# Moving a batch's transposes from the MLP's first half to the output product, with norm statistics as separate steps and a reordered first batch

## The chip, the cores and the metric

The kernel runs on one core of one Trainium2 chip (trn2). The metric is device time in microseconds (us) of one execution. Engines are named as in the profile: PE is TensorE, PEld its weight loads, DVE is VectorE, ACT is ScalarE, POOL is GpSimd. "PEclk" is the granted TensorE clock, where 1.00 is full speed. Most executions of one kernel agree to a few tenths of a per cent. A few are slow: of the kernel before, one took 393.4 us. Only fast runs are compared here.

## The reference, cut to what matters

Dilated sliding-window attention over 8 batches and 8 heads is followed by a gated MLP with a spatial gating unit. Heads 0 to 3 look at the last 32 positions ("plain" heads), and heads 4 to 7 at every fourth of the last 128 ("dilated" heads).

```python
# q, k, v: [8 batches, 8 heads, 576, 64]
scores = scale * q @ k.T;  scores = where(masks, scores, -1e9)
attn = softmax(scores);    x = (attn @ v)            # -> [8, 576, 512]
h = gelu(x @ w_in)                                   # 512 -> 1024
u, v = h[..., :512], h[..., 512:]
v_n = (v - mean(v)) / sqrt(var(v) + 1e-6) * g_ln     # norm over the 512 features
v_s = einsum('ts,bsd->btd', w_sg, v_n) + b_sg        # mixes the positions of a batch
out = x + (u * v_s) @ w_out
```

`w_sg` mixes all positions, so the gating product of a batch cannot finish before the last rows of `v_n` exist.

## The kernel before

The program is written as a list of steps for each batch. Each engine gets its instructions in the order in which the steps stand, so a text of step names is the schedule. `T` transposes q and k, `S` makes scores, `AV` the weighted values, `X` transposes the attention output, `zv`/`zu` are the MLP's first half for v and u, `vn` the norm, `sgu` the gating product, and `out` the output product. In iteration `p`, attention of batch `p` runs beside the gating and output of batch `p - 1`.

```python
ps = tc.tile_pool(name="ps", bufs=4, space=PSUM)       # four PSUM tiles [128, 2, 512] FP32 for everything
NKT, NPT = 3, 10                                       # buffers for kT and for PT

def a_T(b, g):                        # transposes of one head pair
    pq, pk = psum("pq"), psum("pk")
    ...                               # 12 to 16 matmuls against the identity
    nc.scalar.copy(qT, pq[:, :, 0:HS])
    nc.scalar.copy(k0, pk[0:64, :, 0:HS])
    nc.vector.tensor_copy(k1, pk[64:128, :, 0:HS])     # 0.76 us on DVE

def a_S(b, h):
    ...                                                # scores, then Exp on ACT into PT
    eng = nc.gpsimd if b and h % 4 == 3 else nc.vector # masks of heads 3 and 7 on POOL
    eng.tensor_tensor(PT[:, 0:S], PT[:, 0:S], masks[:, h // 4], AO.mult)

def m_zv(b, i):
    ...                                                # 8 matmuls, Gelu on ACT into vv
    for c in range(n):
        nc.vector.bn_stats(st[:, c, :], vv[:, c, :])
        nc.vector.bn_aggr(mv[:, c, :], st[:, c, :])
    nc.gpsimd.tensor_scalar_add(rs[:, 0:n], mv[:, 0:n, 1:2], 1e-6)
    nc.gpsimd.tensor_tensor(rs[:, 0:n], rs[:, 0:n], mhalf[:, 0:n], AO.pow)

def m_vn(b, i):
    for c, ti in enumerate(tis):
        nc.vector.tensor_scalar(vn[:, ti, :], vv[:, c, :], mv[:, c, 0:1],
                                rs[:, c, :], AO.subtract, AO.mult)
...
    # iteration p; io is a list of loads, spread evenly over the steps of a run
    io = ...                                           # v of batch p + 1
    run("S:0 sgu:0 S:1 S:2 sgu:1 S:3 S:4 sgu:2 S:5 sgu:3 S:6 S:7 gelu", env, io)
    run("AV:0 vd AV:1 out:0 X:0 AV:2 X:1 out:1 AV:3 X:2 T:0 X:3 out:2", env, ...)
    io = LOADS["qk"](p + 2) if p + 2 < B else []
    run("zv:0 T:1 zv:1 vn:0 W:0 T:2 zv:2 vn:1 W:1 zu:0 vn:2 T:3 zu:1 W:2 zu:2 W:3 zu:3 W:4",
        env, io)                                       # W prepares w_sg in iteration 0 only
```

Note that the statistics of `vv` follow each `zv` at once, while `vn` stands one `zv` later. Between them DVE has other work: the next statistics and the casts of kT for the transposes `T:1` and `T:2`. All loads are issued by POOL, which also computes `rs`, the reciprocal standard deviation.

The softmax here doesn't subtract the row's maximum and nothing guards it: scores larger than these inputs give would overflow.

## Time and profile before

| | before |
|---|---|
| median (lowest) of its three fast runs | 290.62 us (288.78) |
| profiled execution: span, mean granted clock | 287.8 us, 0.972 |
| first MLP product of batch 0 | 31.13 us |
| first product of batch 1 | 72.60 us |
| five periods from batch 1 to batch 6 | 158.3 us, so 31.7 each |
| batch 6 to batch 7 (no more loads or transposes) | 31.0 us |
| tail from batch 7's first product to the end | 25.9 us |

I cut the execution at the first product of each batch, the matmul that begins `zv:0`. The distance from one to the next is called the period. From the page of the kernel before come the busy time of each engine and the shares of the chain of work that ended last, by engine.

```profile
PE 234.7 (82%) x2494; PEld 167.4 (58%) x2494; DVE 198.7 (69%) x380; ACT 179.2 (62%) x265; POOL 138.9 (48%) x189
...
DVE 31%; PE 30%; ACT 13%; DMA 10%; POOL 8%; issue 6%; POOLq 0%; ACTq 0%; DVEq 0%
```

The view by windows of the kernel before gives the same stretches as the table. The columns are: start and end, length, busy us and number of instructions of PE, PEld, DVE, ACT and POOL, then the granted clock, the DMA share and GB/s.

```profile
0.00:31.13 31.13, 15.34 (x189) 13.80 (x189) 19.89 (x51) 15.41 (x24) 22.65 (x33) 0.92 1.44 147
31.13:72.60 41.47, 33.77 (x340) 22.89 (x339) 27.43 (x49) 22.59 (x34) 23.00 (x32) 0.90 1.26 140
72.60:230.90 158.30, 139.06 (x1543) 99.43 (x1541) 118.11 (x216) 111.56 (x165) 83.95 (x111) 1.00 0.85 101
230.90:261.93 31.03, 27.01 (x299) 19.41 (x297) 22.08 (x43) 21.25 (x31) 5.94 (x8) 1.00 0.11 39
261.93:287.80 25.87, 19.55 (x135) 11.90 (x132) 11.22 (x23) 8.43 (x12) 3.37 (x6) 0.96 0.15 52
```

In the third row PE is busy for 139 of 158 us (88%) at full clock. It is the fullest engine, but not always busy, and DVE leads the chain.

In the timeline of DVE, batch 3 of the kernel before, each line is start, duration, engine, line, operation, operands and count. In brackets stand the idle time before it and what ended that.

```profile
140.77 0.76 DVE L224 CAST kT<-pk 64x576 f16<-64x576 f32 x1
141.56 0.69 DVE L324 BATCH_NORM_STATS2 st<-vv 128x6 f32<-128x512 f32 x1
...
143.19 0.97 DVE L334 TENSOR_SCALAR vn<-vv,mv,rs 128x512 f16<-128x512 f32 x2
144.19 0.81 DVE L224 CAST kI<-pk 64x576 f16<-64x576 f32 x1
...
148.66 0.55 DVE L334 TENSOR_SCALAR vn<-vv,mv,rs 128x512 f16<-128x512 f32 x1 [1.46 <-POOL rs L327]
...
150.11 0.46 DVE L250 TENSOR_TENSOR PT<-PT,masks 128x576 f16<-128x576 f16 x1
```

The kT casts at 140.77 and 144.19 and the second statistics at 141.56 fill the time in which POOL computes `rs`. Only the last `vn` waits (1.46 us), because POOL was issuing four loads, from 144.68 to 147.7, before that `rs`. It runs at 148.66, 12.66 us after the batch's first product at 136.00. The timeline of PE in the same stretch shows what depends on it.

```profile
136.00 1.89 PE L315 MATMUL pz<-w_in,xT 128*128 128x512 f16 x8
...
149.26 0.91 PE L357 MATMUL pv<-wsgT,vn 128*128 128x288 f16 x6 [1.09 <-DVE vn L334]
...
150.60 1.39 PE L357 MATMUL pv<-wsgT,vn 128*128 128x288 f16 x10
...
157.34 0.81 PE L374 MATMUL po<-w_out,gat 128*128 128x512 f16 x3 [0.37 <-DVE vs L361]
```

PE gets to the gating product (`pv`) early, does four of its ten matmuls, and waits 1.09 us for the last `vn`. The output product `po` begins at 157.34, 21.34 us after the first product. The steady batch can be described by three numbers: last `vn` at 12.66, `out:0` at 21.34, next batch at 31.70 us.

### The profile page before, as it was taken

What the parts mean: (1) busy time and instruction counts of PE and PEld (TensorE: products, weight loads), DVE (VectorE), ACT (ScalarE), POOL (GpSimd) and SP (SyncE); (2) the same over time, 40 slices, a digit from 0 to 9 for tenths busy, and PEclk for the clock granted to TensorE, in tenths of its full rate; (3) what the DMA queues carried; (4) which work ended last, traced back from release to release, by engine and by line L of the source; (5) the groups of instructions that cost most, each with busy time, mean ns of one, the idle gap of its engine ahead of it and who ended that gap; (6) DMA issues with size and microseconds to landing.
All of it is one profiled execution on the core that took longest, in us unless ns stands there. A gap on an engine that the chain in (4) does not pass through costs nothing.

```text
span 287.8 us, 6135 instructions
## 1 busy us (share of the span) xinstructions
PE 234.7 (82%) x2494; PEld 167.4 (58%) x2494; DVE 198.7 (69%) x380; ACT 179.2 (62%) x265; POOL 138.9 (48%) x189
## 2 busy tenths in 40 slices
PE   0467957898889798888889898879889889888883
PEld 0366634766468466666567656756566647754652
DVE  7548347795579839794679748993879557973760
ACT  1366643656786478756787478665876678745502
POOL 8953828481188606890198407970396013200400
PEclk9998777999999999999999999999999999999998
DMA  9999999998169921997079923995099310012004
GB/s 129 133 190 150 155 183 108 103 107 151 53 43 126 184 99 8 95 159 171 18 48 156 156 93 25 108 147 155 16 69 164 122 57 2 2 73 93 0 0 164
DMA packets 91467, 28.92 MB, mean 100 GB/s; under 512 B 71664, under 2 KB 86064, under 8 KB 91440
## 3 DMA queue, kind: packets, MB, share of 16 engines
q0 software_dynamic: 85232, 18.48, 72.3%
q1 hardware_dynamic: 6208, 10.06, 10.3%
q8 instruction: 19, 0.31, 0.4%
q14 instruction: 8, 0.07, 0.1%
HBM read 37.54 MB, written 9.44 MB: 163 GB/s over the span
## 4 chain that ended last, share of the span: by engine, by line
DVE 31%; PE 30%; ACT 13%; DMA 10%; POOL 8%; issue 6%; POOLq 0%; ACTq 0%; DVEq 0%
PE po L374 8%; PE pu L344 8%; DVE vs L361 7%; PE pz L315 7%; DVE gat L364 5%; DVE st L324 5%; DMA w_in<-in_moe_w_in_dram 4%; DVE PT L250 4%; DMA wsg<-in_moe_w_sg_dram 4%; DVE onorm L273 3%; ACT vv L319 3%; POOL kp L123 2%; ACT u L347 2%; PE po L377 2%; ACT osb L380 2%
## 5 line engine op out<-in xcount | busy, mean ns | idle before, releaser
L326 POOL TENSOR_SCALAR rs<-mv 128x2 f32<-128x2 f32 (+1 forms) x24 | 7.2, 300 | 96.8 <-DVE mv L325 96.1
L357 PE MATMUL pv<-wsgT,vn 128*128 128x288 f16 x320 | 45.4, 286 | 7.3 <-DVE vn L334 6.3
L247 ACT ACTIVATE PT<-pss 128x576 f16<-128x576 f32 x64 | 38.5, 650 | 16.5 <-PE pss L243 9.9
L374 PE MATMUL po<-w_out,gat 128*128 128x512 f16 x160 | 42.6, 379 | 5.6 <-DVE gat L364 3.0
L324 DVE BATCH_NORM_STATS2 st<-vv 128x6 f32<-128x512 f32 x40 | 27.2, 681 | 25.2 <-ACT vv L319 24.8
L315 PE MATMUL pz<-w_in,xT 128*128 128x512 f16 x160 | 39.9, 392 | 5.6 <-DVE kT L224 5.6
L380 ACT COPY osb<-po 128x1024 f32<-128x1024 f32 (+1 forms) x24 | 20.9, 870 | 37.4 <-issue 20.9
L357 PEld LDWEIGHTS <-vn 128*128 128x128 f16 x320 | 29.0, 97 | 16.2 <-DVE vn L334 8.6
L344 PE MATMUL pu<-xT,w_in 128*128 128x288 f16 x256 | 35.7, 294 | 2.6 <-ACT u L347 1.6
L344 PEld LDWEIGHTS <-w_in 128*128 128x128 f16 x256 | 25.7, 100 | 11.6 <-issue 3.7
L334 DVE TENSOR_SCALAR vn<-vv,mv,rs 128x512 f16<-128x512 f32 x40 | 22.1, 584 | 13.8 <-POOL rs L327 13.8
L273 DVE TENSOR_TENSOR onorm<-poa,rc 96x768 f16<-96x768 f32 (+1 forms) x32 | 30.6, 956 | 1.1
L319 ACT ACTIVATE vv<-pz 128x1024 f32<-128x1024 f32 (+1 forms) x24 | 21.1, 882 | 14.0 <-PE pz L315 11.6
L347 ACT ACTIVATE u<-pu 128x576 f16<-128x576 f32 x32 | 20.8, 651 | 13.2 <-PE pu L344 13.1
L123 POOL DMA_DIRECT2D qp<-in_q_dram x32 | 25.1, 786 | 6.8 <-DMA wsg<-in_moe_w_sg_dram 3.7
L215 ACT CAST qT<-pq 128x576 f16<-128x576 f32 x32 | 20.4, 638 | 12.3 <-PE pq L204 6.4
L123 POOL DMA_DIRECT2D kp<-in_k_dram x32 | 23.9, 752 | 7.8 <-DMA w_in<-in_moe_w_in_dram 4.1
L315 PEld LDWEIGHTS <-xT 128*128 128x128 f16 x160 | 15.3, 101 | 20.9 <-issue 7.5
L361 DVE SCALAR_TENSOR_TENSOR vs<-pv,g_col,b_bc 128x576 f16<-128x576 f32 x32 | 25.9, 811 | 1.2 <-PE pv L357 1.0
L250 POOL TENSOR_TENSOR PT<-PT,masks 128x576 f16<-128x576 f16 x14 | 17.8, 1273 | 18.2 <-ACT PT L247 18.2
L374 PEld LDWEIGHTS <-gat 128*128 128x128 f16 x160 | 14.4, 100 | 18.9 <-DVE gat L364 7.2
L250 DVE TENSOR_TENSOR PT<-PT,masks 128x576 f16<-128x576 f16 x50 | 21.9, 452 | 4.1 <-ACT PT L247 3.3
(65 smaller groups left out, 442.1 us busy)
## 6 DMA issues: line engine op xcount, KB each, us to landing
out_dram<-osb SPq DMA_DIRECT2D x32, 256.0 KB, 2.3
qp<-in_q_dram POOLq DMA_DIRECT2D x32, 72.0 KB, 3.9
kp<-in_k_dram POOLq DMA_DIRECT2D x32, 72.0 KB, 3.4
qd<-in_q_dram POOLq DMA_DIRECT2D x8, 288.0 KB, 5.5
kd<-in_k_dram POOLq DMA_DIRECT2D x8, 288.0 KB, 6.5
vp<-in_v_dram POOLq DMA_DIRECT2D x8, 288.0 KB, 8.4
vm<-in_v_dram POOLq DMA_DIRECT2D x8, 256.0 KB, 6.5
vt<-in_v_dram POOLq DMA_DIRECT2D x16, 96.0 KB, 6.1
```

Source lines behind the costliest of these rows:

```text
L123: nc.gpsimd.dma_start(dst, src)
L247: nc.scalar.activation(PT[:, 0:S].rearrange("p (j w) -> p j w", j=2), pss[:, :, 0:HS], AF.Exp, scale=0.125)
L250: eng.tensor_tensor(PT[:, 0:S], PT[:, 0:S], masks[:, h // 4], AO.mult)
L273: nc.vector.tensor_tensor(onorm.rearrange("p a h d -> p h a d"), pv[:, :, :, 0:64], rc.unsqueeze(3).broadcast_to([rows, 2, NB, 64]), AO.mult)
L315: nc.tensor.matmul(pz[:, c, :], xT[:, g4, MT[ti]:MT[ti] + 128], w_in16[:, g4, DH:DFF], start=(g4 == 0), stop=(g4 == 3))
L319: nc.scalar.activation(vv[:, 0:n], pz[:, 0:n], AF.Gelu_apprx_tanh)
L324: nc.vector.bn_stats(st[:, c, :], vv[:, c, :])
L344: nc.tensor.matmul(pu[:, j, 0:HS], w_in16[:, g4, 128 * ph:128 * ph + 128], xT[:, g4, HS * j:HS * j + HS], start=(g4 == 0), stop=(g4 == 3))
L357: nc.tensor.matmul(pv[:, j, 0:HS], vn[:, kp, 128 * ph:128 * ph + 128], wsgT16[:, kp, HS * j:HS * j + HS], start=(kp == 0), stop=(kp == 4))
L361: nc.vector.scalar_tensor_tensor(vs.rearrange("p (j w) -> p j w", j=2), pv[:, :, 0:HS], g_col[:, ph:ph + 1], b_bc.rearrange("p (j w) -> p ...
L374: nc.tensor.matmul(po[:, c, :], gat[:, ph, ts], w_out16[:, ph, :], start=(ph == 0), stop=False)
L380: nc.scalar.copy(osb[:, 0:n], po[:, 0:n])
```

## The change

The intent has four parts. All transposes of the next batch move out of the MLP's first half and stand beside the output product. The statistics become a step of their own (`st`), so that DVE's order can be chosen freely. Batch 0 begins with the dilated heads, whose load is one large transfer each for q and k. Loads become named steps, and three masks per batch (heads 0, 2, 4) go to POOL instead of two. Some buffers are reduced too (`NKT` and `NPT` in the cut, and `xT` from four to two); e14_best3 below keeps these fewer buffers and is faster than the kernel before, so they alone do not make a kernel slow.

```diff
-    NKT = 3
+    NKT = 2
-    NPT = 10
+    NPT = 8
...
-        dma(w_in16, moe_w_in.rearrange("(g p) f -> p g f", p=128))
+        for half in (slice(DH, DFF), slice(0, DH)):
+            dma(w_in16[:, :, half], moe_w_in[:, half].rearrange("(g p) f -> p g f", p=128))
...
-        eng = nc.gpsimd if b and h % 4 == 3 else nc.vector
+        eng = nc.gpsimd if b and h in (0, 2, 4) else nc.vector
...
+        norm[b, i] = (vv, tis)
+
+    def m_st(b, i):                       # bn_stats, bn_aggr, and rs on POOL, moved here
+        vv, tis = norm.pop((b, i))
...
-    for f, *a in LOADS["qk"](0) + LOADS["v"](0):
+    for f, *a in [(ld_dil, 0), (ld_vd, 0), (ld_plain, 0, 0), (ld_plain, 0, 2),
+                  (ld_vp, 0, 0, 4), (ld_win,), (ld_plain, 1, 0), (ld_plain, 1, 2), (ld_dil, 1)]:
...
+            run("""T0:2 T0:3 S:4 S:5 S:6 S:7 vd T0:0 AV:2 T0:1 AV:3 S:0 X:2 S:1 X:3 S:2 S:3
+                   AV:0 AV:1 gelu X:0 X:1
+                   zv:0 zv:1 st:0 vn:0 zv:2 st:1 vn:1 st:2 wsg LV LVd wout zu:0 vn:2 zu:1 T:0 zu:2
+                   T:1 zu:3 T:2 W:0 W:1 T:3 W:2 W:3 W:4""", env)          # iteration 0
...
-        run("S:0 sgu:0 S:1 S:2 sgu:1 S:3 S:4 sgu:2 S:5 sgu:3 S:6 S:7 gelu", env, io)
-        run("AV:0 vd AV:1 out:0 X:0 AV:2 X:1 out:1 AV:3 X:2 T:0 X:3 out:2", env, io)
-        run("zv:0 T:1 zv:1 vn:0 W:0 T:2 zv:2 vn:1 W:1 zu:0 vn:2 T:3 zu:1 W:2 zu:2 W:3 zu:3 W:4",
-            env, io)
+        run("S:0 S:1 sgu:0 S:2 S:3 sgu:1 S:4 S:5 sgu:2 S:6 sgu:3 S:7 gelu", env)
+        if p == 1:
+            for f, *a in [(ld_plain, 2, 0), (ld_plain, 2, 2), (ld_dil, 2)]:
+                f(*a)
+        run("vd AV:0 LV AV:1 T:0 out:0 X:0 AV:2 LVd X:1 T:1 out:1 AV:3 X:2 T:2 LD X:3 T:3 out:2", env)
+        run("zv:0 st:0 zv:1 vn:0 st:1 zv:2 vn:1 st:2 zu:0 vn:2 LP:0 zu:1 LP:2 zu:2 zu:3", env)
```

In the new text, `LP` and `LD` load q and k of batch `p + 2` (plain heads, dilated heads), and `LV` and `LVd` load v of batch `p + 1`.

More of the change, by code (lines that the diff above doesn't have):

```diff
@@ L108, in setup_consts @@
         nc.sync.dma_start(masks, MSK.ap())
-        nc.vector.memset(mhalf, -0.5)
         for i in range(NKT):
@@ L112, in setup_consts @@
                 nc.vector.memset(kTs[i][hd], 0.0)
-            nc.vector.memset(kIs[i], 0.0)
-        for t in vps + vds:
-            nc.vector.memset(t[0:HALO], 0.0)
-            nc.vector.memset(t[:, :, :, 64:65], 1.0)
+        for t in kIs:
+            nc.vector.memset(t, 0.0)
+        for i in range(NV):
+            nc.vector.memset(vps[i][0:HALO, 0, 0, 0:D], 0.0)
+            nc.vector.memset(vps[i][:, :, :, D:D + 1], 1.0)
+            nc.vector.memset(vds[i][:, :, :, D:D + 1], 1.0)
         for t in PTb:
             nc.vector.memset(t[:, S:PTW], 1.0)
+        nc.vector.memset(mhalf, -0.5)
         nc.vector.memset(wsgT16[0:64, 4, :], 0.0)
@@ L127, in open_batch @@
     def open_batch(b):
+        if b in loaded:
+            return
         qp = ld.tile([QB, NB, 4, D], FP16, tag="qp", name="qp")
@@ L134, in ld_plain @@
     def ld_plain(b, h0):
-        if h0 == 0:
-            open_batch(b)
+        open_batch(b)
         for t, src in zip(loaded[b][0], (q, k)):
@@ L141, in ld_dil @@
     def ld_dil(b):
+        open_batch(b)
         for t, src in zip(loaded[b][1], (q, k)):
@@ L279, in a_X @@
         onorm = onorms.pop((b, g))
-        if g == 0:
-            xTs[b] = sb.tile([128, 4, S], FP16, tag="xT", name="xT", bufs=4)
+        if b not in xTs:
+            xTs[b] = sb.tile([128, 4, S], FP16, tag="xT", name="xT", bufs=2)
         xT = xTs[b]
@@ L319, in m_zv @@
         nc.scalar.activation(vv[:, 0:n], pz[:, 0:n], AF.Gelu_apprx_tanh)
+        norm[b, i] = (vv, tis)
+    def m_st(b, i):
+        vv, tis = norm.pop((b, i))
+        n = len(tis)
         st = sb.tile([128, 2, 6], FP32, tag="st", name="st", bufs=3)
@@ L387, in gelu_table, with run @@
         nc.scalar.activation(warm, mhalf[:, 0, :], AF.Gelu_apprx_tanh)
-    LOADS = {"qk": lambda b: [(ld_plain, b, 0), (ld_plain, b, 2), (ld_dil, b)],
-             "v": lambda b: [(ld_vp, b, 0, 4), (ld_vd, b)]}
-    def run(text, env, io):
-        steps = text.split()
-        done = 0
-        for i, step in enumerate(steps):
-            while done < len(io) and done * len(steps) <= i * len(io):
-                f, *a = io[done]
-                f(*a)
-                done += 1
+    def run(text, env):
+        for step in text.split():
             name, _, n = step.partition(":")
@@ L404, in run @@
                 f(*a, *([int(n)] if n else []))
-        for f, *a in io[done:]:
-            f(*a)
     setup_consts()
-    for f, *a in LOADS["qk"](0) + LOADS["v"](0):
+    for f, *a in [(ld_dil, 0), (ld_vd, 0), (ld_plain, 0, 0), (ld_plain, 0, 2),
+                  (ld_vp, 0, 0, 4), (ld_win,), (ld_plain, 1, 0), (ld_plain, 1, 2), (ld_dil, 1)]:
         f(*a)
-    ld_win()
-    for g in range(4):
-        a_T(0, g)
     for p in range(B + 1):
@@ L417 @@
             env |= {"S": (a_S, p), "AV": (a_AV, p), "X": (a_X, p), "vd": (cp_vd, p),
-                    "zv": (m_zv, p), "vn": (m_vn, p), "zu": (m_zu, p)}
+                    "zv": (m_zv, p), "st": (m_st, p), "vn": (m_vn, p), "zu": (m_zu, p)}
         if p + 1 < B:
-            env["T"] = (a_T, p + 1)
-        if p == 0:
-            env["W"] = (prep_wsg,)
+            env |= {"T": (a_T, p + 1), "LV": (ld_vp, p + 1, 0, 4), "LVd": (ld_vd, p + 1)}
+        if p + 2 < B:
+            env |= {"LP": (ld_plain, p + 2), "LD": (ld_dil, p + 2)}
         if p >= 1:
@@ L425 @@
         if p == 0:
-            io = LOADS["qk"](1) + [(ld_wsg,)]
-        else:
-            io = LOADS["v"](p + 1) if p + 1 < B else []
-        run("S:0 sgu:0 S:1 S:2 sgu:1 S:3 S:4 sgu:2 S:5 sgu:3 S:6 S:7 gelu", env, io)
-        io = LOADS["v"](1) + [(ld_wout,)] if p == 0 else []
-        run("AV:0 vd AV:1 out:0 X:0 AV:2 X:1 out:1 AV:3 X:2 T:0 X:3 out:2", env, io)
-        io = LOADS["qk"](p + 2) if p + 2 < B else []
-        run("zv:0 T:1 zv:1 vn:0 W:0 T:2 zv:2 vn:1 W:1 zu:0 vn:2 T:3 zu:1 W:2 zu:2 W:3 zu:3 W:4",
-            env, io)
+            env |= {"T0": (a_T, 0), "W": (prep_wsg,), "wsg": (ld_wsg,), "wout": (ld_wout,)}
+            run("""T0:2 T0:3 S:4 S:5 S:6 S:7 vd T0:0 AV:2 T0:1 AV:3 S:0 X:2 S:1 X:3 S:2 S:3
+                   AV:0 AV:1 gelu X:0 X:1
+                   zv:0 zv:1 st:0 vn:0 zv:2 st:1 vn:1 st:2 wsg LV LVd wout zu:0 vn:2 zu:1 T:0 zu:2
+                   T:1 zu:3 T:2 W:0 W:1 T:3 W:2 W:3 W:4""", env)
+            continue
+        run("S:0 S:1 sgu:0 S:2 S:3 sgu:1 S:4 S:5 sgu:2 S:6 sgu:3 S:7 gelu", env)
[4 more added lines that the diff above has]
+        run("zv:0 st:0 zv:1 vn:0 st:1 zv:2 vn:1 st:2 zu:0 vn:2 LP:0 zu:1 LP:2 zu:2 zu:3", env)
 _INS = ['q', 'k', 'v', 'moe_w_in', 'moe_g_ln', 'moe_w_sg', 'moe_b_sg', 'moe_w_out']
```

## The prediction

> **What bounds the kernel now.** The busy table by windows gives a steady batch (first product to first product) of 31.7 us: PE 27.8, DVE 23.7, ACT 22.3, POOL 17.4 busy. PE leads, but the timeline shows where it waits. Counted from the first MLP matmul of a batch: MLP's first half ends at 11.3; `sgu:0` waits for the last `vn` until 13.2 (idle 1.1); S/sgu ends at 19.7; AV/X/out at 31.7, with DVE working without a break from 14.1 to 26.9, `out:0` waiting for `gat` and `X:1` for `onorm`. Batch 0 reaches its first product at 31 us and batch 1 at 72.8 (chain of waits: DMA of `w_in`, then of `wsg`). Six periods follow (to 262.1), then a 25.7 us tail.
>
> **What the change does.**
> 1. First half without transposes: PE 8.2 us of work instead of 9.8. But DVE's order becomes st0 vn0 st1 vn1 st2 vn2, and each vn waits for POOL's `rs` (add 0.23, pow 0.73, plus hand-over: 1.15 us). Before, st1 and the kT casts covered that. Walk: vv0 at 3.0, st0 4.7, vn0 6.9, st1 8.6, vn1 10.9, st2 11.7, vn2 13.4. So `sgu:0` starts no earlier than today (13.2); PE just idles longer (some 4 us).
> 2. The eight q/k loads LP stand on POOL between the last `rs` (12.8) and the first mask. At 0.73 each POOL is busy until 18.7, then masks h0, h2, h4 at 1.27 each until 22.6. AV:0 waits until about 20, AV:1 until 21.5.
> 3. In the trace, `gat` on DVE takes 1.2 us instead of 0.46 wherever it overlaps a POOL mask. The Trainium skill, "SBUF — State Buffer", section "Who interferes with whom", says that a DVE instruction with two SBUF inputs contends with a GpSimd instruction that reads SBUF; the trace agrees. Three masks in a row will now hold up gat2, gat3 and DVE's own masks, about 1 to 2 us.
> 4. `out:0` now comes after AV:0, AV:1 and T:0, which fill all four PSUM tiles, so it waits for AV:0's onorm, behind `vd` (0.75): 23 without item 3's delays, up to 26.3 with them, against 21.3 today. From there PE needs 10.4 us to the next first product, three more transposes included. Period 33.4 to 36.7 instead of 31.7.
>
> **On the critical path:** items 1 to 4, in the five periods with a full set of loads and transposes: +1.8 to +5 us each. Batch 6 to 7 stays near 31. The tail gains item 1's exposed waits: +3.3.
>
> **Start.** Dilated loads first, AV and X between: first product at about 23 instead of 31. But `wsg` is issued after the last `rs` (about 36), lands near 41.5, and five `W` with DVE evictions follow: the first `sgu` near 47 instead of 53. Batch 2's loads are issued after batch 1's masks, so T:0 waits for them. Batch 1's first product at about 71 (-2).
>
> Sum: 71 + 5 x 35.5 + 31 + 29 = about 309 us, slower by 6%. Range 298 to 321. Faster 0.05, same 0.1, slower 0.85.
>
> **Right if** the windows show steady periods of 33 to 37 us, vn waiting for POOL rs some 1.1 us three times a batch, the first mask on POOL starting behind the qp/kp issues, PE idle before `sgu:0` and before `out:0`, and the first product near 23. Longer PE idleness may also lower the clock: before, matmuls ran at about half speed around 42 to 50 us after such a gap (the skill's "TensorE: Matmul & The Clock Gate", Part 1, gives an idle window as cause).
>
> **Wrong if** DVE covers the rs waits, POOL's issues are cheaper than 0.73 us, PSUM tiles come free in another order, or the 8 us gained at the start survive `wsg` and steady batches stay under 32.5.

## More of the kernel before

The groups of waits in the kernel before have the columns total us, times and longest us.

```profile
DVE vn L334 <- POOL rs L327: 13.8, 8, 5.5
...
PE pv L357 <- DVE vn L334: 6.3, 7, 1.1
```

## The result, and the profile after

The changed kernel is correct and took 332.05 us (median of four fast runs, 331.36 to 332.86) against 290.62 us for the kernel before (median of its three fast runs, 288.78 to 291.59; the fourth was the slow one). The ratio is 1.144, with a 95% interval of 1.136 to 1.152. Here and below, a ratio is the mean time of one kernel's fast runs over that of the other's of the same rounds, so it is not quite the ratio of the medians that are quoted. The direction was predicted; the size was not (309, 298 to 321).

The page and the windows of the changed kernel follow, with the columns as before.

```profile
PE 251.3 (76%) x2494; PEld 175.9 (53%) x2494; DVE 205.0 (62%) x366; ACT 179.4 (54%) x265; POOL 146.3 (44%) x197
...
DVE 40%; PE 23%; ACT 12%; POOL 9%; DMA 7%; issue 7%; POOLq 0%; ACTq 0%; DVEq 0%
```

```profile
0.00:28.35 28.35, 13.09 (x176) 11.53 (x177) 15.82 (x44) 14.21 (x22) 18.42 (x28) 1.00 1.40 143
28.35:80.21 51.86, 37.52 (x398) 27.01 (x396) 29.27 (x50) 27.12 (x41) 27.81 (x36) 0.80 0.96 100
80.21:266.47 186.26, 151.43 (x1544) 105.82 (x1542) 126.82 (x210) 111.84 (x166) 90.80 (x118) 0.94 0.77 92
266.47:299.49 33.02, 26.88 (x255) 18.39 (x253) 21.58 (x39) 17.85 (x26) 6.58 (x9) 0.95 0.10 36
299.49:331.10 31.61, 22.33 (x135) 13.19 (x132) 11.53 (x23) 8.42 (x12) 2.67 (x6) 0.85 0.13 43
```

| stretch | before | after | difference | predicted for after |
|---|---|---|---|---|
| start to batch 0's first product | 31.1 | 28.4 | -2.8 | 23 |
| batch 0 to 1 | 41.5 | 51.9 | +10.4 | 48 |
| five periods, batch 1 to 6 | 158.3 | 186.3 | +28.0 | 177.5 |
| batch 6 to 7 | 31.0 | 33.0 | +2.0 | 31 |
| tail | 25.9 | 31.6 | +5.7 | 29 |
| whole span | 287.8 | 331.1 | +43.3 | 309 |

The five full periods carry two thirds of the loss. In them PE ran practically the same number of instructions (1,544 against 1,543), but was busy for 151 instead of 139 us at a clock of 0.94 instead of 1.00, and idle for 35 instead of 19 us. The groups of waits show what PE waited for.

```profile
DVE vn L344 <- POOL rs L337: 26.4, 24, 1.2
...
PE pv L367 <- DVE vn L344: 24.7, 21, 3.0
```

Every one of the 24 `rs` computations is now waited for, 1.1 us each. Before, 8 were. Behind it, PE's wait for `vn` grew from 6.3 to 24.7 us. The timeline of DVE in batch 5 of the changed kernel (first product at 230.13) shows the new order.

```profile
236.03 1.00 DVE L344 TENSOR_SCALAR vn<-vv,mv,rs 128x512 f16<-128x512 f32 x2 [1.16 <-POOL rs L337]
...
239.78 1.00 DVE L344 TENSOR_SCALAR vn<-vv,mv,rs 128x512 f16<-128x512 f32 x2 [1.13 <-POOL rs L337]
...
242.61 0.55 DVE L344 TENSOR_SCALAR vn<-vv,mv,rs 128x512 f16<-128x512 f32 x1 [1.01 <-POOL rs L337]
...
246.47 0.99 DVE L255 TENSOR_TENSOR PT<-PT,masks 128x576 f16<-128x576 f16 x1 [0.45 <-ACT PT L252]
...
249.09 1.27 DVE L255 TENSOR_TENSOR PT<-PT,masks 128x576 f16<-128x576 f16 x1 [0.18 <-ACT PT L252]
...
251.74 1.53 DVE L255 TENSOR_TENSOR PT<-PT,masks 128x576 f16<-128x576 f16 x1
```

Each `vn` pair (x2) directly follows its own statistics, so DVE stands still while POOL computes `rs`: 1.16, 1.13 and 1.01 us. The last `vn` is at 242.61, 12.48 us after the first product. That is no later than before (12.66). But before, DVE also made the kT casts and PE made three of the four transposes in that time; now both still have them to do. The last three lines are masks on DVE, 0.99, 1.27 and 1.53 us instead of 0.46 (as at 150.11 in the kernel before). The timeline of POOL in the same batch shows what ran beside them.

```profile
234.96 0.23 POOL L336 TENSOR_SCALAR rs<-mv 128x2 f32<-128x2 f32 x1 [13.44 <-DVE mv L335]
235.27 0.72 POOL L337 TENSOR_TENSOR rs<-rs,mhalf 128x2 f32<-128x2 f32 x1
...
242.51 1.71 POOL L125 DMA_DIRECT2D qp<-in_q_dram  x2
...
248.53 4.41 POOL L255 TENSOR_TENSOR PT<-PT,masks 128x576 f16<-128x576 f16 x3
```

The first two lines are the pair that makes `rs` (0.23 and 0.72 us). The loads of q and k for the plain heads then take POOL from 242.51 to 248.53, and only then come the three masks, 4.41 us together. The timeline of PE completes the batch.

```profile
230.13 4.48 PE L320 MATMUL pz<-w_in,xT 128*128 128x512 f16 x20
...
243.21 1.46 PE L367 MATMUL pv<-wsgT,vn 128*128 128x288 f16 x6 [2.08 <-DVE vn L344]
...
245.43 2.08 PE L367 MATMUL pv<-wsgT,vn 128*128 128x288 f16 x10
...
254.05 0.41 PE L209 MATMUL pk<-ident,kp 96*128 96x96 f16 x6 [1.52 <-DVE vs L371]
254.30 1.03 PE L384 MATMUL po<-w_out,gat 128*128 128x512 f16 x4
```

The gating product restarts at 243.21, and ten of its matmuls take 2.08 instead of 1.39 us. PE runs slower after the wait: the view by windows gives a granted clock of 0.64 from 243.2 to 248 us, and 1.00 before that. The output product begins at 254.30, 24.17 us after the first product. PE had waited 1.52 us before the second half of transpose `T:0`, which the trace ascribes to DVE's `vs`. The matmuls of `pk` do not read `vs`, so this must have been a PSUM tile that came free only when DVE had read the last gating product.

In batch 6 of the same kernel, the output product is followed by no transposes, since batch 7 is the last. It begins at 289.25 us, and batch 7's first product at 299.49. One line of the PE timeline:

```profile
289.25 0.81 PE L384 MATMUL po<-w_out,gat 128*128 128x512 f16 x3
```

From `out:0` to the next first product it is thus 10.24 us there, against 12.17 in batch 5 (254.30 to 266.47). The view by windows has PE busy for 8.37 us in the one stretch and for 10.32 in the other, at a clock of 1.00 in both.

At the start (PE timeline of the changed kernel, two lines of it), PE could begin when the transfer of `qd` landed at 9.48 us, and later it stood 8.04 us for `wsg`.

```profile
9.48 0.66 PE L216 MATMUL pq<-ident,qd 72*128 72x72 f16 x8 [9.48 <-DMA qd<-in_q_dram]
...
49.41 1.14 PE L191 MATMUL pw<-ident,wsg 96*128 96x96 f16 x12 [8.04 <-DMA wsg<-in_moe_w_sg_dram]
```

### The profile page after: what moved, and what is told of

Read it like the earlier page. It is cut to its first block, busy times and chain, and to the rows that moved or that the text cites. A ratio compares the mean times of both kernels' runs of the same rounds, so it can differ in the third digit from the quotient of the medians.

```text
span 331.1 us, 6140 instructions
## 1 busy us (share of the span) xinstructions
PE 251.3 (76%) x2494; PEld 175.9 (53%) x2494; DVE 205.0 (62%) x366; ACT 179.4 (54%) x265; POOL 146.3 (44%) x197
## 4 chain that ended last, share of the span: by engine, by line
DVE 40%; PE 23%; ACT 12%; POOL 9%; DMA 7%; issue 7%; POOLq 0%; ACTq 0%; DVEq 0%
DVE st L334 8%; PE pv L367 7%; DVE PT L255 6%; DVE vn L344 6%; PE po L384 6%; DVE vs L371 6%; DMA kd<-in_k_dram 5%; POOL rs L337 5%; PE pz L320 5%; DVE gat L374 4%; DVE onorm L278 4%; ACT vv L324 2%; DVE mv L335 2%; DMA wsg<-in_moe_w_sg_dram 2%; ACT osb L390 2%
## 5 line engine op out<-in xcount | busy, mean ns | idle before, releaser
L367 PE MATMUL pv<-wsgT,vn 128*128 128x288 f16 x320 | 58.8, 333 | 25.2 <-DVE vn L344 24.7
L336 POOL TENSOR_SCALAR rs<-mv 128x2 f32<-128x2 f32 (+1 forms) x24 | 5.4, 223 | 137.2 <-DVE mv L335 137.2
L367 PEld LDWEIGHTS <-vn 128*128 128x128 f16 x320 | 33.9, 113 | 41.5 <-DVE vn L344 29.7
L384 PE MATMUL po<-w_out,gat 128*128 128x512 f16 x160 | 44.3, 399 | 5.5 <-ACT xT L306 3.1
L320 PE MATMUL pz<-w_in,xT 128*128 128x512 f16 x160 | 37.5, 390 | 0.3 <-ACT xT L294 0.3
L255 DVE TENSOR_TENSOR PT<-PT,masks 128x576 f16<-128x576 f16 x43 | 34.8, 809 | 3.9 <-ACT PT L252 3.3
L255 POOL TENSOR_TENSOR PT<-PT,masks 128x576 f16<-128x576 f16 x21 | 29.1, 1401 | 14.7 <-ACT PT L252 14.6
L354 PE MATMUL pu<-xT,w_in 128*128 128x288 f16 x256 | 33.0, 286 | 0.3 <-ACT u L357 0.3
L371 DVE SCALAR_TENSOR_TENSOR vs<-pv,g_col,b_bc 128x576 f16<-128x576 f32 x32 | 25.9, 810 | 11.8 <-PE pv L367 11.7
L278 DVE TENSOR_TENSOR onorm<-poa,rc 128x768 f16<-128x768 f32 (+1 forms) x32 | 30.6, 955 | 1.1
L229 DVE CAST kI<-pk 64x576 f16<-64x576 f32 x16 | 12.9, 806 | 23.6 <-ACT kI L228 23.6
L357 ACT ACTIVATE u<-pu 128x576 f16<-128x576 f32 x32 | 20.8, 650 | 9.8 <-PE pu L354 9.8
L125 POOL DMA_DIRECT2D qp<-in_q_dram x32 | 24.7, 781 | 1.9 <-DMA kd<-in_k_dram 1.5
L320 PEld LDWEIGHTS <-xT 128*128 128x128 f16 x160 | 15.5, 100 | 18.7 <-issue 1.6
```

What stands on the lines that cost most here:

```text
L125: nc.gpsimd.dma_start(dst, src)
L278: nc.vector.tensor_tensor(onorm.rearrange("p a h d -> p h a d"), pv[:, :, :, 0:64], rc.unsqueeze(3).broadcast_to([rows, 2, NB, 64]), AO.mult)
L320: nc.tensor.matmul(pz[:, c, :], xT[:, g4, MT[ti]:MT[ti] + 128], w_in16[:, g4, DH:DFF], start=(g4 == 0), stop=(g4 == 3))
L354: nc.tensor.matmul(pu[:, j, 0:HS], w_in16[:, g4, 128 * ph:128 * ph + 128], xT[:, g4, HS * j:HS * j + HS], start=(g4 == 0), stop=(g4 == 3))
L367: nc.tensor.matmul(pv[:, j, 0:HS], vn[:, kp, 128 * ph:128 * ph + 128], wsgT16[:, kp, HS * j:HS * j + HS], start=(kp == 0), stop=(kp == 4))
L371: nc.vector.scalar_tensor_tensor(vs.rearrange("p (j w) -> p j w", j=2), pv[:, :, 0:HS], g_col[:, ph:ph + 1], b_bc.rearrange("p (j w) -> p ...
```

## The experiments

The theory to be tested said that the main cost is DVE's order, which exposes the `rs` wait three times in a batch. Its rivals were: the loads on POOL that hold up the masks; the lower PE clock after the waits; the place of the transposes beside the output product; and, for the first batch alone, the late load of `w_sg`. All fourteen kernels gave correct results.

Of the expectations, those of e1_stats, e13_before_T3 and e14_best3 gave the time, and that of e8_mix gave the total but not the first product of batch 1. e5_stats_lp came out just above its range. The rest missed. The times of e2_lp, e3_warm, e6_stats_mask, e7_before_T, e11_best and e12_best2 came out as their rivals had it, those of e4_wsg and e9_before_T2 fell between theory and rival, and e10_after_T2 was slower than its range.

The table gives three times of one full batch (batch 5, from its own first product), read from the PE and DVE timelines. The last column is the time from the last `vn` to the next batch's first product. It separates what is lost in the norm chain from what is lost behind it.

| kernel | last `vn` | `out:0` | next batch | behind the last `vn` |
|---|---|---|---|---|
| before | 12.65 | 21.34 | 31.5 | 18.9 |
| after | 12.48 | 24.17 | 36.3 | 23.9 |
| e1_stats | 9.53 | 21.41 | 33.9 | 24.4 |
| e2_lp | 12.48 | 25.60 | 37.0 | 24.5 |
| e5_stats_lp | 9.54 | 19.75 | 31.2 | 21.7 |
| e7_before_T | 9.53 | 22.61 | 36.1 | 26.6 |
| e9_before_T2 | 9.53 | 19.99 | 34.4 | 24.8 |
| e13_before_T3 | 9.53 | 18.13 | 31.3 | 21.8 |
| e14_best3 | 9.53 | 19.74 | 31.2 | 21.7 |

### One thing undone at a time

**e1_stats** gives DVE the next statistics before each `vn`, in batches 1 to 7. Nothing else is changed.

```diff
-run("zv:0 st:0 zv:1 vn:0 st:1 zv:2 vn:1 st:2 zu:0 vn:2 LP:0 zu:1 LP:2 zu:2 zu:3", env)
+run("zv:0 st:0 zv:1 st:1 vn:0 zv:2 st:2 vn:1 zu:0 vn:2 LP:0 zu:1 LP:2 zu:2 zu:3", env)
```

> The changed kernel with one edit for batches 1 to 7: DVE's order in MLP's first half is st0 st1 vn0 st2 vn1 vn2 (as before the change) instead of st0 vn0 st1 vn1 st2 vn2. Theory A (each vn waits 1.0 to 1.2 us for POOL's rs with nothing to do, PE stands before sgu:0 and cools down): the last vn ends about 10 us after the batch's first product instead of 13, seven batches are 2 to 4 us shorter each, 332 becomes 305 to 318. Rival B (the transposes moved beside the output product, and POOL's loads before the masks, set the period): the first mask on POOL also comes some 2.5 us earlier since the loads start behind the last rs, but if B is right PE only waits later and the gain is under 7 us.

Measured: 306.66 us, ratio to the kernel before of the same rounds 1.058 (1.051 to 1.064), clock of the profiled run 0.955. The change of one line took back 25 of the 41 us. The timeline of DVE in its batch 5 (first product 217.10) shows the norm, and two later operations that matter further down.

```profile
223.48 0.97 DVE L344 TENSOR_SCALAR vn<-vv,mv,rs 128x512 f16<-128x512 f32 x2
...
225.19 0.97 DVE L344 TENSOR_SCALAR vn<-vv,mv,rs 128x512 f16<-128x512 f32 x2
226.63 0.55 DVE L344 TENSOR_SCALAR vn<-vv,mv,rs 128x512 f16<-128x512 f32 x1 [0.47 <-POOL rs L337]
...
230.06 1.25 DVE L374 TENSOR_TENSOR gat<-u,vs 128x576 f16<-128x576 f16 x1
231.24 1.52 DVE L255 TENSOR_TENSOR PT<-PT,masks 128x576 f16<-128x576 f16 x1
```

Two `vn` no longer wait, the third waits 0.47 us. The last one moved from 12.48 to 9.53, by 2.95 us, and the period fell from 36.3 to 33.9. The time behind the last `vn` stayed nearly the same (23.9 and 24.4). So the norm chain lies on the critical path: of its 2.95 us, 2.4 came through to the period. The slower PE went with it: the 200 gating matmuls of the five periods were busy for 35.7 us in the changed kernel, for 28.7 here and for 28.6 in the kernel before. The remaining batches gained as well: 33.0 to 28.3 from batch 6 to 7, and 31.6 to 25.9 in the tail.

**e2_lp** leaves DVE's order as changed and moves the loads of plain q and k behind the masks on POOL.

```diff
-run("vd AV:0 LV AV:1 T:0 out:0 X:0 AV:2 LVd X:1 T:1 out:1 AV:3 X:2 T:2 LD X:3 T:3 out:2", env)
+run("vd AV:0 LV AV:1 T:0 out:0 X:0 AV:2 LVd X:1 T:1 out:1 AV:3 X:2 T:2 LD LP:0 LP:2 X:3 T:3 out:2", env)
-run("... zu:0 vn:2 LP:0 zu:1 LP:2 zu:2 zu:3", env)
+run("... zu:0 vn:2 zu:1 zu:2 zu:3", env)
```

> The changed kernel with the eight q/k loads of the batch after next (LP) issued by POOL beside the last transposes instead of between the last rs and the first mask. If these 5.8 us of issue before the masks are on the critical path as the prediction said: the first POOL mask starts when its exp is done (11 us after the first product instead of 18.4), DVE's masks no longer stand behind three POOL masks in a row, and batches 1 to 5 get 1.5 to 3 us shorter: 332 becomes 317 to 325. Rival: DVE and the late sgu:0 set the pace, masks on POOL have slack: under 4 us gain.

Measured: 334.42 us, ratio 1.153 (1.149 to 1.157), clock 0.892. There was no gain at all. With POOL free, its first mask now starts right behind the last `rs`, while DVE begins the last `vn`. First the POOL timeline, then the DVE timeline of this kernel.

```profile
243.36 1.28 POOL L255 TENSOR_TENSOR PT<-PT,masks 128x576 f16<-128x576 f16 x1
```

```profile
243.44 1.48 DVE L344 TENSOR_SCALAR vn<-vv,mv,rs 128x512 f16<-128x512 f32 x1 [1.01 <-POOL rs L337]
```

The last `vn` took 1.48 us beside the mask instead of 0.55. That delays the gating product, which then runs slower still (ten of its matmuls took 2.60 us in this batch, against 2.08 in the changed kernel). The Trainium skill, "SBUF — State Buffer", section "Who interferes with whom", says that `tensor_scalar` can take a mode that uses the port pair shared with GpSimd and then contends with it; this pair of lines agrees.

**e3_warm** keeps PE awake: 28 matmuls that nothing uses are put ahead of `sgu:0`, into the same PSUM tile, which the real product then overwrites.

```diff
         pv = psum("pv")
+        if ph == 0:
+            for _ in range(28):
+                nc.tensor.matmul(pv[:, 0, 0:HS], ident16, wsgT16[:, 0, 0:HS],
+                                 start=True, stop=True)
```

> The changed kernel with 28 matmuls of no use (128x288 each, about 3.4 us at full clock) into the first pv tile, before sgu:0's own matmuls overwrite it: the result stays right. They run while PE waits for vn. If the lower granted clock (0.914 on average, 0.85 in the tail, against 0.97 and 0.96 before) is a consequence of that wait and costs time by itself: granted clock above 0.96 in batches 2 to 7, sgu:0 to sgu:1 at full speed, and 5 to 12 us off 332 although PE has more to do. Rival: the clock's slow stretches lie in slack: time unchanged within 3 us, or longer by the fillers in batch 1 (up to 3.4).

Measured: 335.09 us, ratio 1.154 (1.145 to 1.163), clock 0.935 instead of 0.914. The five full periods took 189.6 us, three more than without the filler. The cold stretch had moved to the output product, where four matmuls took 1.86 and 1.34 instead of 1.03 us. But where few waits follow, the clock was worth something: the tail fell from 31.6 to 28.8 us and batch 6 to 7 from 33.0 to 31.6. In the tail the gating product restarted 13.1 us after the first product in both kernels, and only then ran faster. So the clock is a true cost at the end of the run. For the full batches, this experiment does not separate it from the waits, since it only moved the cold stretch.

**e4_wsg** loads `w_sg` right after `w_in` instead of after batch 0's norm.

```diff
-                  (ld_vp, 0, 0, 4), (ld_win,), (ld_plain, 1, 0), (ld_plain, 1, 2), (ld_dil, 1)]:
+                  (ld_vp, 0, 0, 4), (ld_win,), (ld_wsg,), (ld_plain, 1, 0), (ld_plain, 1, 2), (ld_dil, 1)]:
-                   ... st:2 wsg LV LVd wout zu:0 ...
+                   ... st:2 LV LVd wout zu:0 ...
```

> The changed kernel with the load of w_sg issued right after w_in, before batch 1's q and k, instead of after the last rs of batch 0. It lands near 31 to 35 us instead of 49.4, so PE's 8 us wait for it ends, but batch 1's q/k land some 4 us later. If that wait is on the critical path: the first sgu (54.7) comes 7 to 10 us earlier and the whole kernel takes 322 to 326. Rival: batch 1's first product waits for batch 2's loads on POOL anyway, gain under 3 us.

Measured: 328.29 us, ratio 1.133 (1.126 to 1.140). Batch 1's first product came at 75.9 instead of 80.2 us. That is 4.3 of the 10.4 us that the stretch from batch 0 to 1 had lost.

### Two things together

**e5_stats_lp** is e1_stats with the loads moved as in e2_lp, the edit of e2_lp made on e1_stats:

```diff
-run("... T:2 LD X:3 T:3 out:2", env)
-run("zv:0 st:0 zv:1 st:1 vn:0 zv:2 st:2 vn:1 zu:0 vn:2 LP:0 zu:1 LP:2 zu:2 zu:3", env)
+run("... T:2 LD LP:0 LP:2 X:3 T:3 out:2", env)
+run("zv:0 st:0 zv:1 st:1 vn:0 zv:2 st:2 vn:1 zu:0 vn:2 zu:1 zu:2 zu:3", env)
```

> The changed kernel with both edits: DVE's order st0 st1 vn0 st2 vn1 vn2 (306.7 alone) and LP moved behind the masks (334.4 alone, no gain: there the first POOL mask ran into the last vn, which took 1.48 us instead of 0.55, and the late vn set the pace). With the vn early, the first mask should start some 4 us earlier than with the order alone (11.4 instead of 15.5 us after the first product) without touching vn, DVE's gat and masks should wait less for POOL, and the period should fall from 33.9 to 31 to 32.5: 290 to 299 in all. Rival: LP's place is worth nothing in any order: 304 to 309.

Measured: 299.47 us, ratio 1.034 (1.029 to 1.039). The same move that was worth nothing alone is worth about 7 us here (306.66 to 299.47; the two ran in different rounds, beside 289.9 and 289.7 us of the kernel before). The full period fell from 33.9 to 31.2 us, a little below the 31.7 of the kernel before. The table says where: `out:0` moved from 21.41 to 19.75. The PE timeline of e1_stats shows what stood there, though not POOL's masks themselves:

```profile
233.54 1.39 PE L367 MATMUL pv<-wsgT,vn 128*128 128x288 f16 x10 [1.39 <-DVE vs L371]
```

PE waited for DVE's `vs` (1.39, then 0.69 and 0.88 us in that batch), because DVE's `gat` and masks before it took 1.25 and 1.52 us beside POOL's loads and masks. Here the slowest of these took 1.10 us, and the waits for `vs` shrank to one of 0.41 us. Batch 1 to 2 was still 39.2 us: in batch 1 POOL issued loads of batches 2 and 3, and waited between them for earlier transfers, until 91.3 us, and only then came the first `rs`; `vn` waited 5.02 us for it.

**e6_stats_mask** is e1_stats with the POOL masks of the kernel before.

```diff
-        eng = nc.gpsimd if b and h in (0, 2, 4) else nc.vector
+        eng = nc.gpsimd if b and h % 4 == 3 else nc.vector
```

> The changed kernel with DVE's order as before and the masks of heads 3 and 7 on POOL (as before the change) instead of 0, 2 and 4; LP stays between rs and the masks. If three POOL masks in a row behind LP, with DVE's two-input instructions blocked beside them, are what holds the period at 33.9: the first POOL mask is then wanted only when LP is done, the long masks on DVE (1.52 us instead of 0.45, two per batch) go, period 31.5 to 33, in all 292 to 301. Rival: the six masks on DVE instead of five cost as much as that saves: 304 to 309.

Measured: 308.31 us, ratio 1.066 (1.060 to 1.071), periods of 32.8 to 34.0 us. DVE's `gat` now took up to 1.64 us. Choosing other heads for POOL gives nothing while the loads stand in front of the masks.

### The transposes by themselves, in the kernel before

**e7_before_T** is the kernel before with only the transposes moved.

```diff
-run("AV:0 vd AV:1 out:0 X:0 AV:2 X:1 out:1 AV:3 X:2 T:0 X:3 out:2", env, io)
+run("AV:0 vd AV:1 T:0 out:0 X:0 AV:2 X:1 T:1 out:1 AV:3 X:2 T:2 X:3 T:3 out:2", env, io)
-run("zv:0 T:1 zv:1 vn:0 W:0 T:2 zv:2 vn:1 W:1 zu:0 vn:2 T:3 zu:1 W:2 zu:2 W:3 zu:3 W:4",
+run("zv:0 zv:1 vn:0 W:0 zv:2 vn:1 W:1 zu:0 vn:2 zu:1 W:2 zu:2 W:3 zu:3 W:4",
```

> The kernel before with only one part of the change: all transposes of the next batch beside the output product (none left in MLP's first half). Its DVE order there is st0 st1 vn0 st2 vn1 vn2 already. Theory: this part is not what costs the time; the last vn comes at 10 us after the first product instead of 13.2, and period 30.5 to 31.9, in all 282 to 292. Rival B: transposes beside the output product fill the PSUM tiles and hold up PE: period 33 or more, 298 or more.

Measured: 311.16 us, ratio 1.073 (1.070 to 1.077), clock 0.921. I had thought that the transposes were harmless once the norm was early, and expected 282 to 292 us. That expectation failed. The norm did get early (last `vn` at 9.53), but the time behind it grew from 18.9 to 26.6 us. The timeline of PE around the output product of batch 4 shows two waits.

```profile
203.19 0.64 PE L204 MATMUL pq<-ident,qp 96*128 96x96 f16 x6 [2.04 <-DVE vs L361]
...
205.79 1.89 PE L374 MATMUL po<-w_out,gat 128*128 128x512 f16 x4 [1.48 <-DVE onorm L273]
```

`T:0` waits 2.04 us for DVE, and behind it `out:0` waits 1.48 us for the `onorm` of `AV:0`, since `AV:0`, `AV:1` and `T:0` hold all four PSUM tiles. The four matmuls then take 1.89 us where a warm PE takes 1.03. This is the mechanism that the prediction gave for the changed kernel.

**e9_before_T2** puts `T:0` behind `X:0`, so that `out:0` finds a free PSUM tile. It is e7_before_T with one step moved.

```diff
-run("AV:0 vd AV:1 T:0 out:0 X:0 AV:2 X:1 T:1 out:1 AV:3 X:2 T:2 X:3 T:3 out:2", env, io)
+run("AV:0 vd AV:1 out:0 X:0 T:0 AV:2 X:1 T:1 out:1 AV:3 X:2 T:2 X:3 T:3 out:2", env, io)
```

> The kernel before with all transposes beside the output product, as in the run that took 311.2, but T:0 stands after out:0 and X:0 instead of before them. In that run out:0 waited 1.5 us for AV:0's onorm (not its input: it must have been the PSUM tile), after T:0 had waited 2.0 us for vs3, and PE then ran out:0 at half speed. If the place of T:0 (two more PSUM tiles taken before out:0) is the cause, out:0 starts when gat3 is there and the period falls from 36 to 31 to 32.5: 282 to 295 in all. Rival: transposes beside the output product cost the time wherever they stand (casts on DVE and ACT between the onorms): 304 or more.

Measured: 302.0 us, ratio 1.043 (1.039 to 1.047). `out:0` moved from 22.6 to 20.0, and 9 us of the 21 were won back. What remained: masks and `gat` on DVE took 1.01, 1.25, 1.52 and 1.07 us instead of 0.46, while POOL issued loads of q, k and v and did its masks in between, and `out:0` waited 2.04 us for the last `vs`.

**e13_before_T3** therefore also moves the q and k loads of later batches into the run of the output product, behind the masks.

```diff
-io = LOADS["v"](1) + [(ld_wout,)] if p == 0 else []
+io = LOADS["v"](1) + [(ld_wout,)] if p == 0 else LOADS["qk"](p + 2) if p + 2 < B else []
 run("AV:0 vd AV:1 out:0 X:0 T:0 AV:2 ...", env, io)
-io = LOADS["qk"](p + 2) if p + 2 < B else []
+io = LOADS["qk"](2) if p == 0 else []
```

> The kernel before with all transposes beside the output product, T:0 behind X:0 (302.0), and now from batch 1 on the q/k loads issued by POOL beside the output product, behind its masks, instead of in MLP's first half. In the 302 run gat and the masks on DVE took 1.0 to 1.5 us instead of 0.46 four times a batch beside POOL's issues and masks, 3 us together. If that collision is the cause and not the transposes, the period falls from 34.4 to 30.5 to 32: 280 to 292 in all. Rival: the casts of the moved transposes between the onorms: 298 or more.

Measured: 290.25 us, ratio 1.002 (0.997 to 1.007). Full periods are 31.3 to 33.0 us, 28.3 from batch 6 to 7, and the tail is unchanged. In batch 5, the 1.25 and 1.52 us on DVE are gone; two `gat` of 1.01 and 1.08 us beside POOL's masks remain. The transposes beside the output product thus cost 21 us where they come with the PSUM wait and with POOL's loads before the masks, and this place can be had for nothing. That the transposes are neutral by themselves is not shown: the kernel before with only the loads moved was not run, and it might be faster, since its last `vn` waited 1.46 us behind these loads.

**e10_after_T2** makes the move of `T:0` in the changed kernel.

```diff
-run("vd AV:0 LV AV:1 T:0 out:0 X:0 AV:2 LVd ...", env)
+run("vd AV:0 LV AV:1 out:0 X:0 T:0 AV:2 LVd ...", env)
```

> The changed kernel with only T:0 moved behind out:0 and X:0. Theory: in the changed kernel the late vn and the masks set when gat3 comes (24 us after the first product), and out:0 waited no more than 0.5 us for anything else, so this is worth 0 to 8 us: 324 to 332. Rival: the place of T:0 is a main cause here too: under 318.

Measured: 337.27 us, ratio 1.163 (1.158 to 1.168), from fast runs of 335.82 to 338.5. Its profiled run was slow (342.94 us), so I read no detail from its trace. I had expected 324 to 332. The place of `T:0` is not what holds the changed kernel up: while `vn` is late, the move brings nothing, and costs a little (ratio 1.163 against 1.144, with intervals that do not overlap). Why it costs is open.

### Put together

**e8_mix** takes only the start of the change, with `w_sg` early and batch 2's loads at the end of batch 0, and goes on with the schedule of the kernel before. The cut diff, against the kernel before:

```diff
...                                   # start, buffers, m_st and batch 0 as in the changed kernel
+                  (ld_vp, 0, 0, 4), (ld_win,), (ld_wsg,), (ld_plain, 1, 0), (ld_plain, 1, 2), (ld_dil, 1)]:
+                   zv:0 zv:1 st:0 st:1 vn:0 zv:2 st:2 vn:1 LV LVd wout zu:0 vn:2 zu:1 T:0 zu:2
+                   T:1 zu:3 T:2 W:0 W:1 T:3 W:2 W:3 W:4 LP:0 LP:2 LD""", env)
...                                   # later batches: the old order, loads as steps
+        run("LV S:0 sgu:0 S:1 S:2 sgu:1 S:3 S:4 sgu:2 LVd S:5 sgu:3 S:6 S:7 gelu", env)
+        run("AV:0 vd AV:1 out:0 X:0 AV:2 X:1 out:1 AV:3 X:2 T:0 X:3 out:2", env)
+        run("LP:0 zv:0 st:0 T:1 zv:1 st:1 vn:0 T:2 LP:2 zv:2 st:2 vn:1 zu:0 vn:2 T:3 LD zu:1 zu:2 zu:3", env)
```

> The start of the changed kernel (dilated heads first), with w_sg loaded right after w_in and batch 0's statistics in the old DVE order, and from batch 1 on the schedule of the kernel before (transposes, masks, loads, order). If the changed start is good in itself and only its late w_sg and its loads of batch 2 behind batch 1's masks spoiled it: batch 1's first product at 62 to 68 us instead of 72.6, steady periods of 31.7, 279 to 286 in all. Rival: the changed start is no better (72 or later): 290 or more.

Measured: 285.49 us, ratio 0.985 (0.981 to 0.990), clock 0.979. First products of batches 0 and 1 at 28.8 and 69.8 us instead of 31.1 and 72.6 (62 to 68 had been expected for batch 1); later periods 31.6 to 31.7 as before. The start of the change is a gain of about 3 us once `w_sg` does not come late.

**e11_best** keeps all of the change and repairs what was found: the statistics' order in all batches, the loads behind the masks, `w_sg` early, and batch 2's loads at the end of batch 0. The diff is against the changed kernel.

```diff
+                  ... (ld_win,), (ld_wsg,), ...
-                   zv:0 zv:1 st:0 vn:0 zv:2 st:1 vn:1 st:2 wsg LV LVd wout zu:0 vn:2 zu:1 T:0 zu:2
-                   T:1 zu:3 T:2 W:0 W:1 T:3 W:2 W:3 W:4""", env)
+                   zv:0 zv:1 st:0 st:1 vn:0 zv:2 st:2 vn:1 LV LVd wout zu:0 vn:2 zu:1 T:0 zu:2
+                   T:1 zu:3 T:2 W:0 W:1 T:3 W:2 W:3 W:4 LP:0 LP:2 LD""", env)
-        if p == 1:
-            for f, *a in [(ld_plain, 2, 0), (ld_plain, 2, 2), (ld_dil, 2)]:
-                f(*a)
...                                   # the two runs of later batches as in e5_stats_lp
```

> The changed kernel with four repairs: DVE's order st0 st1 vn0 st2 vn1 vn2 in all batches, LP behind the masks, w_sg loaded right after w_in, batch 2's q and k loaded at the end of batch 0 instead of behind batch 1's masks. Sum of what was measured: batch 1's first product at 69.8 us as in the mixed kernel, five periods of 31.2, one of 28.3, tail 26: about 280, that is 272 to 285 and faster than before (289.7). Rival: the early loads and LP together overrun the DMA queue in batches 1 and 2 (POOL waits for the queue), and 5 to 8 us are lost again: 286 or more.

Measured: 288.63 us, ratio 0.996 (0.991 to 1.001). The full periods are 31.2 us, but batch 0 to 1 took 46.4: batch 1's `AV` waited 2.35 and 0.5 us for POOL masks that stood behind batch 2's loads. This collision of two repairs is most of why the expected sum of single results (280) did not come true: without it, e14_best3 takes 282.65.

**e12_best2** is e11_best with `T:0` behind `X:0`, the same edit as in e10_after_T2.

```diff
-run("vd AV:0 LV AV:1 T:0 out:0 X:0 AV:2 LVd ...", env)
+run("vd AV:0 LV AV:1 out:0 X:0 T:0 AV:2 LVd ...", env)
```

> The same with T:0 behind out:0 and X:0. If T:0 ahead of out:0 still costs something there (pk waited 0.4 us for vs3, out:0 0.6 us for qT per batch), periods of 30 to 31 and 3 to 6 us less than the kernel without this edit. Rival: X:0 and AV:2 then wait for onorm instead: no difference within 2 us.

Measured: 287.98 us, ratio 0.995 (0.991 to 1.000). It cannot be told from e11_best.

**e14_best3** is e11_best with batch 1's masks left on DVE.

```diff
-        eng = nc.gpsimd if b and h in (0, 2, 4) else nc.vector
+        eng = nc.gpsimd if b > 1 and h in (0, 2, 4) else nc.vector
```

> The repaired kernel (288.6) with all masks of batch 1 on DVE; POOL takes masks from batch 2 on. There AV:0 and AV:1 of batch 1 waited 2.35 and 0.5 us for POOL's masks, which stood behind batch 2's loads, and out:0 then 2.6 us for onorm. If that is the 5 us, batch 1's first product comes at 69 to 72 instead of 74.4 and the whole takes 282 to 286. Rival: DVE is busy all the time there and the masks on it cost what the waits save: 287 to 290.

Measured: 282.65 us (282.07 to 284.0), ratio 0.976 (0.969 to 0.983), clock 0.979. It is faster than both kernels. Whether it is faster by over 2% the interval leaves open. Batch 0 to 1 fell from 46.4 to 41.2 us. Against the kernel before, the profiled span went from 287.8 to 281.4 us: 2.4 us at the start (batch 1 at 70.2 instead of 72.6), 1.3 in the five full periods, 2.8 from batch 6 to 7, and nothing in the tail. One wait for `rs` of 0.47 us remains in each full batch.

## Why the prediction was wrong

The direction and most of the mechanisms were right; the sum was 23 us short. No single step carried all of that. Each term of the sum was too small: the first product by 5.3 us, batch 0 to 1 by 3.9, the five periods by 8.8, batch 6 to 7 by 2.0, and the tail by 2.6.

- **Item 1, the norm order, was right, to within half a microsecond.** It gave the last `vn` 13.4 us after the first product; its start was read at 12.48 and its end at 13.0. The waits were 1.16, 1.13 and 1.01 us against 1.15. It also said that `sgu:0` would start no earlier than today. Its matmuls resumed at 13.1 against 13.3, so that was right as well. What I did not draw from it is that this item is the main cause: undoing it won 25 of 41 us (e1_stats). I compared `vn` with the kernel before, where it was just as late. But there, three transposes were already done by then; here they were still to come, and only an earlier `vn` could have paid for them.
- **Items 2 and 3 were right as facts, and wrong as terms of a sum.** The first POOL mask came 18.4 us after the first product (18.7 predicted), and DVE masks beside POOL took up to 1.53 us. But "AV:0 waits until about 20" held in time only (20.8 us in batch 5): over the whole run, the `AV` matmuls waited only 2.1 us for POOL's masks. The place of the loads alone is worth nothing (e2_lp), and together with the early norm it is worth about 7 us (e5_stats_lp). Costs that hide behind one another do not add.
- **Item 4 had the right time for `out:0` by luck, with the wrong reason for this kernel.** `out:0` came at 24.2 us, inside the predicted 23 to 26.3. It did not wait for `AV:0`'s onorm; the transpose `T:0` before it waited 1.52 us for DVE's `vs`. The onorm wait that I described appears in e7_before_T (1.48 us).
- **The step that failed in the steady periods is "From there PE needs 10.4 us to the next first product, three more transposes included".** It needed 12.2 to 14.2 us. The 10.4 is what the stretch took in the kernel before (31.70 - 21.34 = 10.36), where one transpose stood in it instead of three. So the work of the added transposes was left out: PE was busy for 9.08 us of that stretch before, and for 10.3 us of the 12.2 in the periods of 36.2 and 36.3 us; the rest of the growth is waits. Without transposes, in batch 6 of the same kernel, it took 10.24 us. In the two longest periods (38.5 and 38.4 us) the clock came on top: the stretch took 14.2 and 13.1 us at a granted clock of 0.88 and 0.87, and in the first of them groups of four output matmuls took 1.76 and 1.80 us instead of 1.03. Over the five periods this term was 12.1 us too small (64.1 against 52), and `out:0` came 3.3 us earlier in sum than the period of 35.5 implies, which leaves the 8.8 us.
- **The clock was named as a risk and left out of the sum.** In the tail, 36 gating matmuls took 7.49 instead of 4.58 us, so 2.9 us, about the error there. e3_warm agrees: with a warmer PE the tail was 2.8 us shorter. e3_warm could not show what the clock costs in the full periods; that the gating matmuls were busy there for 7.1 us more than before (35.7 against 28.6) bounds only this one part of it.
- **Start: the first product was expected at 23 and came at 28.35.** The record does not say how the 23 was made up, so the step that failed in it stays open. The runs show that the dilated `qd` and `kd` landed at 9.48 and 11.7 us, and that matmuls ran slow until about 22 us (six transposing matmuls took 0.67 us there and 0.42 later), although the view gives a granted clock of 1.00 for this stretch. `wsg` was issued at 42.62 rather than 36 (5.3 us of this is the late first product) and landed at 49.41 rather than 41.5, so the first gating product came at 54.7 rather than 47. e4_wsg shows what the late issue is worth, 4.3 us.
- **"Right if the windows show steady periods of 33 to 37 us"**: they were 36.2 to 38.5, three of the five within it. "vn waiting for POOL rs some 1.1 us three times" held in every batch.

What stays open:

- Why DVE operations with two inputs take 1.25 to 1.52 us in stretches where POOL only issues loads. In e1_stats, `gat` at 230.06 and the mask at 231.24 were slow, and the POOL timeline of the same kernel shows loads until 232.56, so all of the first and nearly all of the second ran beside loads only:

```profile
231.10 1.45 POOL L125 DMA_DIRECT2D kp<-in_k_dram  x2
232.56 4.23 POOL L255 TENSOR_TENSOR PT<-PT,masks 128x576 f16<-128x576 f16 x3
```

  Yet a mask at 228.72 took 0.46 us beside the same kind of issues.
- The order in which the four PSUM tiles come free.
- Why some periods of e13_before_T3 are 33.0 us and others 31.3.
- What else keeps the first product at 27.6 to 29.6 us in every kernel with the changed start.

## What to carry to other kernels

Before work is moved out of a stage, look at what it was covering. Here the next statistics, with the casts of the transposes, filled the wait for a small operation on another engine. The new order put nothing in their place and exposed the wait three times per batch; the next statistics alone would have covered two of the three (e1_stats). When several waits end near the same moment, test the repairs together as well as alone: one of them was worth nothing alone and 7 us with the other. A good idea in one part of a change (the start, here) should be measured apart from the rest, since the sum of the change hid it completely.

## What the Trainium skill lacked or had wrong

- "SBUF — State Buffer", "Who interferes with whom": it says that a DVE instruction with two SBUF inputs contends with a GpSimd instruction that reads SBUF, and the traces agree (masks of 1.27 and 1.53 us beside POOL masks, 0.46 alone, while `vs`, with one input in PSUM, kept its 0.8 us beside them). It also infers that a `tensor_tensor` takes only the pair's read interface, while descriptor generation needs the write interface, so load issues should not slow it. In e1_stats a `gat` took 1.25 us while POOL only issued loads, and in the changed kernel the mask at 246.47 took 0.99 us beside loads alone. Why is open; the inference does not cover it.
- "TensorE: Matmul & The Clock Gate", Part 1: it puts the fall of the clock after an idle window of about 3.4 us. Here ten gating matmuls took 2.08 instead of 1.39 us after a stretch from 238.9 to 243.2 us in which the longest single gap was 2.08 us, with a few matmuls in between. PE was busy for 1.0 us of these 4.3, and the granted clock was 0.64 in the next 4.8 us. A figure for how much idle time in short pieces lets the clock fall would have helped the sum.
- "DMA: Bandwidth & Descriptors", "Anatomy of one DMA — SWDGE (gpsimd) path": an estimate by its fit (2.0 us plus size over 436 GB/s) gives 2.7 us for the 288 KB of a dilated q transfer. In these traces the median from issue to landing was 8.5 us, with many small packets and other transfers in flight (5.5 us in the kernel before).
- I found no page with the cost of a small POOL pair and its hand-over to DVE. Here add and power took 0.23 and 0.72 us, and DVE stood 1.16 us.
